# Holding the magnitudes of the first MLP's weights within bounds on GpSimd instead of VectorE

## The chip, the cores and the metric

The program runs on one core of one Trainium2 chip. The metric is the device time of one execution in microseconds; the kernel before has a median of 866.44 us (three runs, 866.27 to 866.68). All times below are microseconds unless they are marked ns.

## The reference

Attention over a window of 64 positions (4 batches, 8 heads, 576 positions, 64 numbers per head), then two MLPs of 512 to 2048 to 512 over the 2304 tokens, with a float32 result. The weights are float64; the kernel gets each number as two 32-bit words and makes float32 of them.

```python
scores = np.where(mask, scale * q @ k.T, -1e9)       # mask: 0 <= row - column < 64
attn = exp(scores - max) / (sum + 1e-9);  x = attn @ v
h = x @ moe_w_in;   x = max(h, 0)**2 @ moe_w_out
h = x @ moe2_w_in;  out = (max(h, 0) + log1p(exp(-abs(h)))) @ moe2_w_out
```

## The kernel before

The attention is cut into 18 pairs of 128 tokens. The first MLP works on five token tiles (384, 384, 512, 512, 512), the second on three of 768. A matmul in full precision is made of three passes: operands are split into a high part and the remainder (a ScalarE copy that rounds, then a VectorE subtraction), and high by high, remainder by high and high by remainder are summed.

The first two tiles of the first MLP use the weights directly, 16 chunks f of w_in and 16 of w_out. A block "L1" (function l1, lines 841 to 844) is the 12 matmuls of one chunk of w_in on one tile, a block "K" (line 863) the 12 of one chunk of w_out. TensorE takes L1 of tile 0, K of tile 0, L1 of tile 1 and the attention's matmuls in a written order. The later tiles use sums of quarter matrices (line 1074) that are loaded back from DRAM.

Every chunk of weights is made ready by add_weights, once for each matrix half f and kind (0 for w_in, 1 for w_out), in eight jobs: load (DMA), magnitude on ScalarE (line 498: absolute value of the upper words as floats), hold on VectorE (line 501: minimum with HUGE, maximum with TINY, in place on the tile z, 128x512), shift (505), top (511), bottom (517), all VectorE, then hi on ScalarE (524) and lo on VectorE (528), which leaves the weight tile w ready for TensorE. Tile names hold f and the kind: w_10_1 is chunk 10 of w_out, w_2_0 chunk 2 of w_in. There are 32 such chunks for the first MLP (ph = 0) and 32 for the second (ph = 1).

The order on each engine is made before anything runs by the class Plan. Each job has an engine with a cost, jobs that it follows, and a due time; due times run backwards from the users and are moved by the table SHIFT, by groups of jobs. A list scheduler then lets each engine take the ready job with the earliest due time, each engine on its own. Some small jobs may go to either of two engines. The engines then run their queues strictly in that order.

Of the kernel before, what the change touches and what calls it, by code (L numbers as in the profile page):

```python
# [16 lines left out]
ALU = mybir.AluOpType  # L17
# [13 lines left out]
    "l0": -0.14, "p0": 71.5, "c0": -0.55, "l1": -0.14, "p1": 54.45, "e1": 0.1, "l2": -0.14, "p2": 74.96, "c2": 0.12,  # L31
    "l3": -0.14, "p3": 100.33, "c3": 0.12, "l4": -0.14, "v4": -0.25, "p4": 135.81, "e4": -0.73, "c4": 0.12,
    "l5": -0.14, "v5": -0.25, "p5": 118.77, "c5": 0.12, "l6": -0.14, "v6": -0.25, "p6": 45.02, "c6": 0.12,
    "l7": -0.14, "v7": -0.96, "p7": 20.52, "c7": 0.12, "l8": -0.14, "v8": -0.25, "p8": 11.17, "c8": 0.12, "l9": -0.14,
    "v9": -0.25, "p9": -4.28, "k9": -0.36, "c9": 0.12, "l10": -0.28, "p10": 37.13, "c10": 0.12, "l11": -0.28,
    "p11": 80.95, "c11": 0.12, "l12": -0.28, "v12": -0.19, "p12": 80.69, "k12": 0.04, "c12": 0.12, "l13": -0.28,
    "v13": -0.19, "p13": 78.46, "c13": 0.12, "l14": -0.93, "v14": -0.19, "p14": 67.37, "c14": 0.12, "l15": 0.28,
    "v15": -0.19, "p15": 96.15, "c15": 0.12, "l16": -0.01, "v16": 1.42, "p16": -38.05, "e16": 1.1, "c16": 0.12,
    "l17": 0.28, "v17": -0.19, "p17": 9.62, "c17": 0.12, "u_0_0": -1.02, "W0_0_0": 154.07, "u_1_0": -1.02,
    "u_0_1": -0.98, "g_0_1": -0.6, "W0_1_0": 193.04, "u_2_0": -1.02, "g_2_0": -2.33, "W0_0_1": 162.23, "u_1_1": -1.02,  # L40
    "g_1_1": -0.6, "u_3_0": -1.02, "g_3_0": -0.6, "u_2_1": -1.02, "g_2_1": -1.24, "W0_1_1": -146.3, "u_4_0": -3.21,
    "g_4_0": -1.24, "W0_0_2": -16.31, "u_3_1": -1.02, "g_3_1": -1.24, "u_5_0": -1.02, "u_4_1": -1.02,
    "W0_1_2": -96.68, "u_6_0": -1.02, "W0_0_3": 160.08, "u_5_1": -1.71, "u_7_0": -1.02, "u_6_1": -1.02,
    "W0_1_3": -72.22, "u_8_0": 0.25, "W0_0_4": 120.95, "u_7_1": -1.02, "u_9_0": -0.43, "u_8_1": -0.43,
    "W0_1_4": -37.64, "u_10_0": -3.02, "W0_0_5": -91.79, "u_9_1": -0.43, "u_11_0": -1.02, "u_10_1": -1.02,
    "W0_1_5": 120.18, "u_12_0": -1.02, "W0_0_6": -5.97, "u_11_1": 0.15, "u_13_0": -1.02, "u_12_1": -1.02,
    "W0_1_6": 230.47, "u_14_0": -0.26, "W0_0_7": 157.36, "u_13_1": -1.02, "u_15_0": -1.02, "u_14_1": -1.02,
    "W0_1_7": 325.52, "u_15_1": -1.02, "S0_0": -110.83, "S0_1": -44.6, "S0_2": -140.65, "S0_3": 152.29,
    "S0_4": -39.95, "S0_5": 9.78, "S0_6": -74.99, "S0_7": 145.26, "L0_0_0": -43.69, "G0_0_0": -0.92, "K0_0_0": 14.31,
    "L0_0_1": -94.54, "G0_0_1": -0.92, "K0_0_1": 123.1, "L0_0_2": 68.92, "G0_0_2": -1.02, "K0_0_2": 33.8,  # L50
    "L0_0_3": 121.83, "G0_0_3": -1.38, "K0_0_3": 162.91, "L0_0_4": 239.43, "G0_0_4": -2.06, "K0_0_4": 162.77,
    "L0_0_5": -95.13, "G0_0_5": -0.92, "K0_0_5": 67.09, "L0_0_6": -81.03, "G0_0_6": -0.41, "K0_0_6": 73.88,
    "L0_0_7": -26.46, "G0_0_7": 26.98, "K0_0_7": 208.31, "R0": -32.49, "L0_1_0": -34.78, "K0_1_0": 86.2,
    "L0_1_1": 167.88, "K0_1_1": -5.89, "L0_1_2": 17.91, "K0_1_2": -27.02, "L0_1_3": 72.74, "G0_1_3": -6.65,
    "K0_1_3": 14.9, "L0_1_4": 92.91, "G0_1_4": 0.05, "K0_1_4": 56.56, "L0_1_5": 77, "G0_1_5": 0.33, "K0_1_5": 336.59,
    "L0_1_6": 22.1, "G0_1_6": 0.33, "K0_1_6": 154.04, "L0_1_7": 173.98, "G0_1_7": -3.34, "K0_1_7": 133.05,
    "R1": 17.25, "W1_0_0": 61.58, "S1_0": 19.49, "W1_1_0": 80.16, "W1_0_1": -9.89, "S1_1": 56.76, "W1_1_1": 102.2,
    "W1_0_2": -7.52, "S1_2": 98.8, "W1_1_2": -30.34, "W1_0_3": -17, "S1_3": -67.82, "W1_1_3": 8.21, "W1_0_4": -103.05,
    "S1_4": 146.2, "W1_1_4": 14.02, "W1_0_5": -17.23, "S1_5": -70.65, "W1_1_5": 72.55, "W1_0_6": -38.03,
    "S1_6": 24.85, "W1_1_6": -19.17, "W1_0_7": 7.38, "S1_7": -55.64, "W1_1_7": 154.65, "X0_2": 10.83, "ri0": -3.61,  # L60
    "ro0": 166.84, "P0_2_0": 5.03, "C0_2_0": -1.56, "G0_2_0": 0.71, "K0_2_0": -20.22, "ri1": 18.82, "ro1": 109.55,
    "P0_2_1": 212, "C0_2_1": -1.48, "K0_2_1": 205.81, "ri2": 25.94, "ro2": 177.03, "P0_2_2": 156.22, "C0_2_2": -1.76,
    "G0_2_2": -4.72, "K0_2_2": 148.43, "ri3": 87.08, "ro3": 141.62, "P0_2_3": 322.35, "C0_2_3": 0.29, "G0_2_3": -4.72,
    "K0_2_3": 57.85, "ri4": 79.03, "ro4": 227.07, "P0_2_4": 99.23, "C0_2_4": 0.22, "G0_2_4": -5.38, "K0_2_4": 114.58,
    "ri5": 59.44, "ro5": 198.08, "P0_2_5": -3.21, "C0_2_5": 0.08, "G0_2_5": -0.09, "K0_2_5": -0.98, "ri6": 88.02,
    "ro6": 182.8, "P0_2_6": 163.84, "C0_2_6": 0.08, "G0_2_6": -0.09, "K0_2_6": 113.09, "ri7": 138.86, "ro7": 138.68,
    "P0_2_7": 263.74, "C0_2_7": 0.08, "G0_2_7": -0.09, "K0_2_7": 181.21, "R2": 54.8, "X0_3": 370.32, "P0_3_7": 39.05,
    "K0_3_7": 179.31, "P0_3_6": 141.27, "C0_3_6": -0.31, "K0_3_6": 37.31, "ri10": 113.65, "P0_3_5": 145.56,
    "K0_3_5": -20.44, "ri11": 40.86, "ro11": 55.48, "P0_3_4": 87.56, "G0_3_4": -1.31, "K0_3_4": 26.13, "ri12": 51.84,
    "ro12": 92.26, "P0_3_3": 148.65, "C0_3_3": 0.38, "G0_3_3": -0.99, "K0_3_3": 76.68, "ri13": 22.67, "ro13": 73.47,  # L70
    "P0_3_2": 257.35, "G0_3_2": -0.25, "K0_3_2": 131.88, "ri14": 113.04, "ro14": 60.62, "P0_3_1": 273.45,
    "C0_3_1": -8.82, "G0_3_1": -0.63, "K0_3_1": 300.68, "ri15": 118.91, "ro15": -13.89, "P0_3_0": 289.5,
    "C0_3_0": -8.88, "G0_3_0": -0.64, "K0_3_0": 212.9, "R3": -62.15, "X0_4": 164.51, "P0_4_0": 46.91, "C0_4_0": 0.05,
    "G0_4_0": -0.05, "K0_4_0": 251.79, "P0_4_1": 7.59, "C0_4_1": 1.64, "G0_4_1": -0.05, "K0_4_1": 147.06,
    "ri18": 112.24, "P0_4_2": 160.66, "C0_4_2": 0.56, "G0_4_2": 0.4, "K0_4_2": 1.32, "ri19": 91.23, "ro19": 5.74,
    "P0_4_3": -12.99, "C0_4_3": 0.68, "G0_4_3": 0.4, "K0_4_3": 67.73, "ri20": 112.66, "ro20": 19.04, "P0_4_4": 143.6,
    "C0_4_4": 0.68, "G0_4_4": 0.09, "K0_4_4": -71.32, "ri21": 117.7, "ro21": 102.77, "P0_4_5": 158.38,
    "C0_4_5": -0.84, "G0_4_5": -0.05, "K0_4_5": -47.88, "ri22": 46.58, "ro22": 63.61, "P0_4_6": 136.85,
    "C0_4_6": -2.13, "G0_4_6": 0.36, "K0_4_6": -52.62, "ri23": 27.7, "ro23": 67.19, "P0_4_7": -119.64,
    "C0_4_7": -4.22, "G0_4_7": 2.59, "K0_4_7": 231.35, "R4": 254.02, "x0": 78.58, "X1_0": 258.41, "ri24": 15.07,  # L80
    "ro24": 58, "P1_0_0": -21.24, "C1_0_0": -0.08, "G1_0_0": -0.08, "K1_0_0": -127.63, "ri25": 102.16, "ro25": 26.91,
    "P1_0_1": -88.26, "C1_0_1": -0.08, "G1_0_1": -0.08, "K1_0_1": -121.22, "ri26": 79.46, "ro26": 72.96,
    "P1_0_2": -133.34, "C1_0_2": -0.42, "G1_0_2": 0.53, "K1_0_2": -52.62, "ri27": 120.66, "ro27": 123.66,
    "P1_0_3": -10.81, "C1_0_3": -0.29, "G1_0_3": -0.29, "K1_0_3": -149.5, "ri28": 82.64, "ro28": 250.42,
    "P1_0_4": -225.28, "C1_0_4": -0.13, "G1_0_4": 0.46, "K1_0_4": 30.76, "ri29": 165.89, "ro29": 237.13,
    "P1_0_5": -200.27, "C1_0_5": -0.32, "G1_0_5": -0.29, "K1_0_5": -124.26, "ri30": 151.82, "ro30": 216.72,
    "P1_0_6": -188.21, "C1_0_6": 0.67, "G1_0_6": -0.29, "K1_0_6": -99.09, "ri31": 72.83, "ro31": 145.11,
    "P1_0_7": -187.94, "C1_0_7": -0.13, "G1_0_7": -4.98, "K1_0_7": 115.18, "x1": 162.42, "X1_1": 175.58,
    "P1_1_7": 52.38, "C1_1_7": -0.29, "G1_1_7": -0.83, "K1_1_7": -135.96, "ri33": -142.49, "P1_1_6": 29.25,
    "C1_1_6": -0.27, "G1_1_6": -1.62, "K1_1_6": -61.31, "ri34": -44.65, "ro34": -103.9, "P1_1_5": 67.4,  # L90
    "C1_1_5": 0.17, "G1_1_5": -1.62, "K1_1_5": -87.06, "ri35": -8.37, "ro35": 187.94, "P1_1_4": 9.88, "C1_1_4": -0.24,
    "G1_1_4": -2.11, "K1_1_4": -54.4, "ri36": 4.75, "ro36": 184.88, "P1_1_3": 77.08, "C1_1_3": -0.9, "G1_1_3": -1.62,
    "K1_1_3": -102.93, "ri37": 143.68, "ro37": 162.68, "P1_1_2": 92.1, "C1_1_2": -0.73, "G1_1_2": -1.06,
# [1428 lines left out]
```

## Time and profile before

| | |
|---|---|
| median of three runs | 866.44 us |
| profiled execution, own time | 868.16 us |
| its span, first to last instruction | 866.4 us |
| TensorE (PE) matmul busy | 850.8 us (98%) |
| VectorE (DVE) busy | 724.2 us (84%) |
| ScalarE (ACT) busy | 616.3 us (71%) |
| GpSimd (POOL) busy | 3.6 us |
| granted TensorE clock, mean | 0.998 |

The profiled execution's own time is 1.7 us above the median, and 1.8 us lie around its span. Busy shares are averages over stages: the first 36 us, in which the attention of the first pairs runs and the first weights arrive, look unlike the rest. A matmul's recorded duration is longer than the spacing of matmuls, since they are pipelined; a block of 12 is read from one block's start to the next one's.

### The profile page before, as it was taken

What the parts mean: (1) busy time and instruction counts of PE and PEld (TensorE: products, weight loads), DVE (VectorE), ACT (ScalarE), POOL (GpSimd) and SP (SyncE); (2) the same over time, 40 slices, a digit from 0 to 9 for tenths busy, and PEclk for the clock granted to TensorE, in tenths of its full rate; (3) what the DMA queues carried; (4) which work ended last, traced back from release to release, by engine and by line L of the source; (5) the groups of instructions that cost most, each with busy time, mean ns of one, the idle gap of its engine ahead of it and who ended that gap; (6) DMA issues with size and microseconds to landing.
All of it is one profiled execution on the core that took longest, in us unless ns stands there. A gap on an engine that the chain in (4) does not pass through costs nothing.

```text
span 866.4 us, 16055 instructions
## 1 busy us (share of the span) xinstructions
PE 850.8 (98%) x5688; PEld 770.1 (89%) x5688; DVE 724.2 (84%) x1389; ACT 616.3 (71%) x1413; POOL 3.6 (0%) x19
## 2 busy tenths in 40 slices
PE   8899999999999999999999999999999999999998
PEld 6699999999988998898999888888889898899896
DVE  6999998798799998899467999999876678776675
ACT  7997776674678676675445888888776678676675
POOL 1000000000000000000000000000000000000000
PEclk9999999999999999999999999999999999999999
DMA  9999866999999899997999999894756551664521
GB/s 214 299 304 368 308 236 213 301 314 312 383 246 334 244 367 289 316 341 260 337 346 353 329 315 335 325 340 153 231 177 205 170 193 40 204 208 161 191 101 73
DMA packets 158575, 225.97 MB, mean 261 GB/s; under 512 B 64544, under 2 KB 115744, under 8 KB 158496
## 3 DMA queue, kind: packets, MB, share of 16 engines
q1 hardware_dynamic: 158496, 224.96, 79.3%
q8 instruction: 45, 0.74, 0.3%
q14 instruction: 34, 0.28, 0.1%
HBM read 169.35 MB, written 55.57 MB: 260 GB/s over the span
## 4 chain that ended last, share of the span: by engine, by line
PE 80%; DVE 8%; DMA 6%; SPq 3%; issue 1%; ACT 1%; DVEq 0%; ACTq 0%
PE acc L863 20%; PE acc L886 20%; PE pa L1074 16%; PE pb L1074 7%; PE pd L1074 5%; PE h L841 2%; PE h L842 2%; PE h L844 2%; SPq L643 2%; PE po L745 2%; DMA raw<-in_moe_w_in_dram 2%; PE pp L726 1%; SPq L474 1%; PE sc L682 1%; DVE gl L914 1%
## 5 line engine op out<-in xcount | busy, mean ns | idle before, releaser
L886 PE MATMUL acc<-ro,gh 128*128 128x512 f32 x576 | 178.9, 391 | 0.0
L886 PEld LDWEIGHTS acc<-ro,gh 128*128 128x128 f32 x576 | 107.2, 188 | 18.6
L863 PE MATMUL acc<-gh,ro 128*128 128x512 f32 x384 | 120.4, 395 | 0.0
L886 PE MATMUL acc<-ro,gl 128*128 128x512 f32 x288 | 113.8, 395 | 0.0
L863 PEld LDWEIGHTS acc<-gh,ro 128*128 128x128 f32 x384 | 69.1, 188 | 13.0 <-issue 0.7
L863 PE MATMUL acc<-gl,ro 128*128 128x512 f32 x192 | 74.9, 390 | 0.0
L914 DVE TENSOR_TENSOR gl<-l,gh 128x384 fp32r<-128x384 f32 x96 | 53.1, 553 | 23.3 <-ACT gh L911 22.4
L911 ACT CAST gh<-l 128x384 fp32r<-128x384 f32 x96 | 48.7, 507 | 24.6 <-DVE l L1261 10.6
L863 PE MATMUL acc<-gh,w 128*128 128x384 f32 x256 | 66.0, 338 | 0.0
L886 PEld LDWEIGHTS acc<-ro,gl 128*128 128x128 f32 x288 | 54.0, 188 | 11.7 <-DVE gl L914 0.3
L1074 PE MATMUL pa<-hxT,ri 128*128 128x384 f32 x288 | 62.0, 336 | 0.0
L1074 PE MATMUL pb<-xT,ri 128*128 128x256 f32 x432 | 60.6, 285 | 0.2 <-DVE wk L1116 0.2
L1257 DVE SCALAR_TENSOR_TENSOR e<-u,e 128x384 f32<-128x384 f32 x96 | 52.8, 550 | 6.2 <-ACT u L1247 6.2
L1074 PEld LDWEIGHTS pb<-xT,ri 128*128 128x128 f32 x432 | 55.9, 191 | 2.0 <-DVE wk L1116 0.4
L1261 DVE TENSOR_TENSOR l<-l,e 128x384 f32<-128x384 f32 x96 | 52.9, 553 | 4.2 <-ACT e L1243 0.5
L1074 PEld LDWEIGHTS pa<-hxT,ri 128*128 128x128 f32 x288 | 51.7, 188 | 2.8
L1252 ACT ACTIVATE l<-u 128x384 f32<-128x384 f32 x96 | 50.3, 524 | 2.7 <-DVE u L1249 1.4
L1074 PE MATMUL pa<-xA,ri 128*128 128x256 f32 (+1 forms) x288 | 51.1, 313 | 0.8 <-ACT c L434 0.6
L1243 ACT ACTIVATE e<-e 128x384 f32<-128x384 f32 x96 | 50.3, 524 | 1.8
L1178 ACT COPY wk<-pa 128x384 f32<-128x384 f32 x72 | 34.2, 475 | 22.8 <-PE pa L1074 22.7
L1074 PEld LDWEIGHTS pa<-xA,ri 128*128 128x128 f32 x288 | 45.3, 189 | 4.1 <-ACT c L434 0.9
L1239 ACT ACTIVATE e<-c 128x384 f32<-128x384 f32 x61 | 31.9, 523 | 23.5 <-DVE c L1186 22.6
(240 smaller groups left out, 2014.1 us busy)
## 6 DMA issues: line engine op xcount, KB each, us to landing
ri<-di SPq DMA_DIRECT2D x126, 512.0 KB, 5.6
ro<-do SPq DMA_DIRECT2D x76, 512.0 KB, 5.4
ri<-di SPq DMA_DIRECT2D x42, 256.0 KB, 3.9
raw<-in_moe_w_in_dram SPq DMA_DIRECT2D x16, 512.0 KB, 9.0
raw<-in_moe_w_out_dram SPq DMA_DIRECT2D x16, 512.0 KB, 6.7
do<-w SPq DMA_DIRECT2D x16, 512.0 KB, 5.3
di<-osa SPq DMA_DIRECT2D x32, 256.0 KB, 6.1
di<-osb SPq DMA_DIRECT2D x32, 256.0 KB, 6.1
```

The source lines that it names most:

```text
L643: nc.sync.dma_start(out=t[done:done + n], in_=src[b, :, s:s + n, :].rearrange("h p d -> p h d"))
L863: nc.tensor.matmul(o, lh, rh, start=n == 0 and k == 0, stop=n == NF - 1 and k == 2)
L886: nc.tensor.matmul(o, lh, rh, start=begins and k == 0, stop=ends and k == 2)
L911: nc.scalar.copy(out=place(j, f"gh{me}", [P, T], F32R), in_=live[src])
L914: nc.vector.tensor_tensor(out=place(j, f"gl{me}", [P, T], F32R), in0=live[src], in1=f32(live[f"gh{me}"]), op=ALU.subtract)
L1074: nc.tensor.matmul(out, w[:, s, c, :], x[k][:, c, :], start=(i == 0 and not on), stop=(i == 5), skip_group_check=on)
L1178: nc.scalar.copy(out=live[f"wk{me}"][:, i], in_=live[f"pa{me}"])
L1239: nc.scalar.activation(out=e, in_=live[src], func=AF.Abs)
L1243: nc.scalar.activation(out=e, in_=e, func=AF.Exp, scale=-1.0)
L1252: nc.scalar.activation(out=live[f"l{me}"], in_=live[f"u{me}"], func=AF.Ln)
L1257: nc.vector.scalar_tensor_tensor(out=e, in0=u, scalar=1.0, in1=e, op0=ALU.subtract, op1=ALU.subtract)
L1261: nc.vector.tensor_tensor(out=live[f"l{me}"], in0=live[f"l{me}"], in1=live[f"e{me}"], op=ALU.add)
```

## The change

The hold of the first MLP's 32 chunks goes to GpSimd, with a planned cost of 1.0; the second MLP's stay on VectorE. The table SHIFT has new numbers throughout, so that all engines' orders change. Lines of the kernel after are 10 or 11 higher than of the kernel before.

```diff
 SHIFT = {
-    "l0": -0.14, "p0": 71.5, "c0": -0.55, "l1": -0.14, "p1": 54.45, "e1": 0.1, "l2": -0.14, "p2": 74.96, "c2": 0.12,
+    "l0": -3.29, "v0": -3.48, "p0": 74.2, "k0": -4.57, "e0": -2.64, "c0": -0.47, "l1": 7.42, "v1": -0.92, "p1": 68.17,
...
         def hold(j):
-            nc.vector.tensor_scalar(out=live[z], in0=live[z], scalar1=HUGE, scalar2=TINY, op0=ALU.min, op1=ALU.max)
+            e = nc.gpsimd if j.who == "POOL" else nc.vector
+            e.tensor_scalar(out=live[z], in0=live[z], scalar1=HUGE, scalar2=TINY, op0=ALU.min, op1=ALU.max)
...
-        add(f"B{me}", {"DVE": 0.34}, hold, [f"A{me}"])
+        add(f"B{me}", {"DVE": 0.34} if ph else {"POOL": 1.0}, hold, [f"A{me}"])
```

VectorE before, where the weights w_9_1 and w_10_1 are made ready (z holds the magnitudes, raw the loaded words, gl the remainder of an activation that a K block reads):

```order
L501 TENSOR_SCALAR z_10_1_1477<-z_10_1_1477 128x512
L914 TENSOR_TENSOR gl_0_9_1487<-prow_13_122,gh_0_9_1481 128x384
L505 TENSOR_SCALAR z_10_1_1477<-z_10_1_1477 128x512
L528 TENSOR_TENSOR w_9_1_1485<-z_9_1_1416,w_9_1_1485 128x512
L511 SCALAR_TENSOR_TENSOR z_10_1_1477<-raw_10_1_1413,z_10_1_1477 128x512
L928 TENSOR_TENSOR area<-area 128x384
L517 SCALAR_TENSOR_TENSOR z_10_1_1477<-raw_10_1_1413,z_10_1_1477 128x512
L505 TENSOR_SCALAR z_14_0_1419<-z_14_0_1419 128x512
L501 TENSOR_SCALAR z_15_0_1507<-z_15_0_1507 128x512
L914 TENSOR_TENSOR gl_0_10_1532<-prow_14_121,gh_0_10_1525 128x384
L511 SCALAR_TENSOR_TENSOR z_14_0_1419<-raw_14_0_835,z_14_0_1419 128x512
L528 TENSOR_TENSOR w_10_1_1530<-z_10_1_1477,w_10_1_1530 128x512
```
Each chunk has its hold (501) and shift (505) on VectorE, and the subtraction of w_10_1 (528) is VectorE's instruction number 200 of the program.

VectorE after, ahead of the same subtraction of w_10_1 (its line is now 539, the shift's 516):

```order
L939 TENSOR_TENSOR area<-area 128x384
L522 SCALAR_TENSOR_TENSOR z_11_1_1454<-raw_11_1_1384,z_11_1_1454 128x512
L925 TENSOR_TENSOR gl_0_10_1492<-prow_14_121,gh_0_10_1488 128x384
L528 SCALAR_TENSOR_TENSOR z_11_1_1454<-raw_11_1_1384,z_11_1_1454 128x512
L516 TENSOR_SCALAR z_10_1_1467<-z_10_1_1467 128x512
L516 TENSOR_SCALAR z_14_0_1482<-z_14_0_1482 128x512
L522 SCALAR_TENSOR_TENSOR z_10_1_1467<-raw_10_1_1337,z_10_1_1467 128x512
L539 TENSOR_TENSOR w_11_1_1512<-z_11_1_1454,w_11_1_1512 128x512
L528 SCALAR_TENSOR_TENSOR z_10_1_1467<-raw_10_1_1337,z_10_1_1467 128x512
L925 TENSOR_TENSOR gl_0_11_1535<-prow_15_120,gh_0_11_1509 128x384
L522 SCALAR_TENSOR_TENSOR z_14_0_1482<-raw_14_0_889,z_14_0_1482 128x512
L539 TENSOR_TENSOR w_10_1_1538<-z_10_1_1467,w_10_1_1538 128x512
```
No hold is left on this engine; the subtraction of w_10_1 is its instruction number 189. Of the instructions up to it, 27 holds are gone, and others have come ahead of it: 4 sums of two weight parts, 4 differences of quarters of them, 2 scalings of q, 3 squares, 1 activation's remainder, and one or two more steps of weights.

GpSimd after, the first holds and the two before and behind w_3_1's:

```order
L397 AFFINE_SELECT masks<-masks 64x64 x12
L512 TENSOR_SCALAR z_2_0_426<-z_2_0_426 128x512
L512 TENSOR_SCALAR z_0_0_464<-z_0_0_464 128x512
L512 TENSOR_SCALAR z_3_0_468<-z_3_0_468 128x512
L512 TENSOR_SCALAR z_1_0_546<-z_1_0_546 128x512
L512 TENSOR_SCALAR z_0_1_613<-z_0_1_613 128x512
L512 TENSOR_SCALAR z_1_1_636<-z_1_1_636 128x512
L512 TENSOR_SCALAR z_2_1_744<-z_2_1_744 128x512
L512 TENSOR_SCALAR z_3_1_776<-z_3_1_776 128x512
L512 TENSOR_SCALAR z_4_0_852<-z_4_0_852 128x512
L512 TENSOR_SCALAR z_10_0_944<-z_10_0_944 128x512
```
GpSimd's queue, which ended with the masks before, now holds 32 of these in the order of the weights; each waits for ScalarE's magnitude, and VectorE's shift of the same chunk waits for it.

TensorE before, where the L1 block of chunk 5 on tile 1 (h_1_5) ends:

```order
L842 MATMUL h_1_5_1464<-xh_1_830,w_5_0_1088 128x384
L844 MATMUL h_1_5_1464<-xl_1_831,w_5_0_1088 128x384 x4
L863 MATMUL acc_0_0_912<-gh_0_8_1411,w_8_1_1460 128x384 x2
L863 MATMUL acc_0_0_912<-gl_0_8_1421,w_8_1_1460 128x384
L863 MATMUL acc_0_1_916<-gh_0_8_1411,w_8_1_1460 128x384 x2
L863 MATMUL acc_0_1_916<-gl_0_8_1421,w_8_1_1460 128x384
```
It stands ahead of the K block of w_8_1.

TensorE after, where that L1 block begins:

```order
L874 MATMUL acc_0_2_789<-gh_0_12_1592,w_12_1_1594 128x384 x2
L874 MATMUL acc_0_2_789<-gl_0_12_1596,w_12_1_1594 128x384
L874 MATMUL acc_0_3_793<-gh_0_12_1592,w_12_1_1594 128x384 x2
L874 MATMUL acc_0_3_793<-gl_0_12_1596,w_12_1_1594 128x384
L852 MATMUL h_1_5_1655<-xh_1_892,w_5_0_1039 128x384
L853 MATMUL h_1_5_1655<-xh_1_892,w_5_0_1039 128x384
```
It now stands behind the K block of w_12_1. Up to the first matmul on w_10_1 TensorE has 20 L1 blocks and 10 K blocks before, and 19 L1 and 10 K after, with the same attention work. Up to the first matmul on w_3_1 it has 9 L1 and 3 K blocks and 25 groups of transpositions before, and 4 L1, 3 K and 24 groups after.

## Rows read from the trace of the kernel before

**Rows 1.** The page: span, busy time of each engine, chain by engine

```profile
span 866.4 us, 16055 instructions
...
PE 850.8 (98%) x5688; PEld 770.1 (89%) x5688; DVE 724.2 (84%) x1389; ACT 616.3 (71%) x1413; POOL 3.6 (0%) x19
...
PE 80%; DVE 8%; DMA 6%; SPq 3%; issue 1%; ACT 1%; DVEq 0%; ACTq 0%
```

**Rows 2.** Stretches: busy us and instructions of each engine, PEclk, DMA share, GB/s

```profile
0.00:14.00 14.00, 11.99 (x134) 9.38 (x138) 6.08 (x13) 7.96 (x26) 3.59 (x19) 1.00 1.08 208
14.00:36.00 22.00, 17.24 (x248) 13.82 (x239) 20.89 (x44) 20.26 (x85) 0.00 (x0) 0.92 1.03 243
36.00:108.00 72.00, 69.77 (x507) 67.29 (x508) 71.84 (x146) 60.48 (x136) 0.00 (x0) 1.00 1.00 332
300.00:600.00 300.00, 297.18 (x1913) 265.86 (x1912) 261.20 (x494) 211.28 (x448) 0.00 (x0) 1.00 0.93 320
```

**Rows 3.** VectorE in order: start us, duration us, line, operation, tiles [idle before <-releaser]

```profile
43.40 0.68 DVE L698 TENSOR_REDUCE nm<-sc 128x4 f32<-128x512 f32 x1
44.00 0.68 DVE L511 SCALAR_TENSOR_TENSOR z<-raw,z 128x512 uint32<-128x512 uint32 x1
44.60 0.42 DVE L501 TENSOR_SCALAR z<-z 128x512 f32<-128x512 f32 x1
44.93 0.68 DVE L517 SCALAR_TENSOR_TENSOR z<-raw,z 128x512 uint32<-128x512 uint32 x1
...
68.03 0.67 DVE L528 TENSOR_TENSOR w<-z,w 128x512 fp32r<-128x512 f32 x1
...
105.74 0.54 DVE L914 TENSOR_TENSOR gl<-prow,gh 128x384 fp32r<-128x384 f32 x1
106.20 0.67 DVE L511 SCALAR_TENSOR_TENSOR z<-raw,z 128x512 uint32<-128x512 uint32 x1
106.81 0.67 DVE L528 TENSOR_TENSOR w<-z,w 128x512 fp32r<-128x512 f32 x1
```

**Rows 4.** The chain in order of time: start us, us, what

```profile
65.58 2.08 PE acc L863 x12
67.66 0.17 PE h L841
...
69.74 2.08 PE acc L863 x12
...
107.62 0.44 PE tq L654 x4
108.06 2.11 PE acc L863 x12
```

**Rows 5.** VectorE in order, the idle times of the start

```profile
6.32 0.69 DVE L434 COPY kT<-tk 128x512 f32<-128x512 f32 x1 [3.30 <-PE tk L654]
8.67 1.29 DVE L698 TENSOR_REDUCE nm<-sc 128x4 f32<-128x512 f32 x2 [1.66 <-PE sc L682]
11.18 0.29 DVE L434 COPY kT<-kT 128x256 f32<-128x256 f32 x1 [1.23 <-PE sc L682]
```

**Rows 6.** GpSimd: groups by line, count | busy us, mean ns of one

```profile
L387 POOL TENSOR_SCALAR_AFFINE_SELECT masks<-masks 64x64 bf16<-64x64 bf16 x12 | 2.5, 236 | 0.3
masks.py:199 POOL TENSOR_SCALAR_AFFINE_SELECT ident<-ident 128x128 f32<-128x128 f32 x1 | 0.3, 292 | 0.1
```

**Rows 7.** Groups of VectorE by line and shape, count | busy us, mean ns of one

```profile
L501 DVE TENSOR_SCALAR z<-z 128x512 f32<-128x512 f32 x53 | 21.6, 414 | 4.7 <-ACT z L498 4.7
L501 DVE TENSOR_SCALAR halvesw<-halvesw 128x512 f32<-128x512 f32 x11 | 4.6, 418 | 0.3 <-ACT halvesw L498 0.2
```

**Rows 8.** TensorE's waits from 300 to 600 us: us in total, times, longest

```profile
PE tq L654 <- DVE k L719: 0.9, 1, 0.9
PE pa L1074 <- ACT c L434: 0.6, 1, 0.6
```

**Rows 9.** A stretch of the start, columns as in rows 2

```profile
30.00:34.00 4.00, 3.55 (x11) 3.04 (x12) 3.97 (x9) 2.48 (x7) 0.00 (x0) 0.57 1.01 323
```

154 rows, old and new, of the table SHIFT are left out of this document.

## The prediction

> **What bounds the kernel now.** The page comes first: TensorE is busy for 98% of the span and makes up 80% of the chain of waits [rows 1]. It does the same matmuls before and after, so the time can move only by stretches in which TensorE waits. The busy times by stretches show where these are: TensorE misses 2.0 us of the first 14, 4.8 from 14 to 36 and 2.2 from 36 to 108 [rows 2], and 2.8 from 300 to 600, which the waits put down to single late tiles [rows 2, 8]. In the same stretches VectorE idles 7.9 us, then 1.1, then 0.2 of 72 [rows 2]. So from 14 us until the first MLP's weights are ready VectorE never rests, and TensorE runs just behind it. The rows of VectorE and of the chain side by side show how close: the subtraction that finishes w_3_1 starts at 68.03 and ends 0.67 later, its K block starts at 69.74; for w_10_1 it is 106.81 + 0.67 = 107.48 against 108.06 [rows 3, 4]. What reaches VectorE ahead of these points later than now, by more than 0.6 to 1.0 us, makes TensorE wait, and nothing behind gives that back. What reaches it sooner is worth little, since TensorE misses only 2.2 of the 72 us there.
>
> **The change part by part.** All durations are start to start, because VectorE begins an instruction before the last one's recorded end. A hold takes 0.33 (44.60 to 44.93; 0.335 over many), a 128x512 operation with two tiles 0.60 (44.00 to 44.60), a 128x384 one 0.46 (105.74 to 106.20) [rows 3]. The trace has 64 holds, 53 + 11 [rows 7]; half of them are the first MLP's and leave VectorE, 32 x 0.33 = 10.6 us.
>
> How much of this helps is read where TensorE waits for VectorE. Up to and with the subtraction of w_10_1 VectorE has 201 instructions before. Summed by kind: 56 of 0.335, 115 of 0.60, 13 of 0.47, 12 reciprocals of 0.20 and five small ones of 1.2 together, 97.7 us; the instruction ends at 107.48, so 9.7 us of that time were idle or start-up. After, it has 190: 33, 124, 17, 12 and four, 97.1 us. The 27 holds that are gone (9.0 us) are nearly made up by the operations that the new order puts ahead of this point. TensorE meanwhile has one L1 block less ahead of it, and a block is 2.08 (67.66 to 69.74) [rows 4], so at its present pace it asks for w_10_1 at 108.06 - 2.08 = 105.98. At w_3_1 the sums are 59.0 us (122 instructions) before and 50.4 (100) after, and TensorE has five L1 blocks and one group of transpositions (0.44) less ahead: it asks at 69.74 - 10.84 = 58.9 [rows 4].
>
> With the same 9.7 us of idle time VectorE finishes w_10_1 at 106.8 and w_3_1 at 60.1, 0.9 and 1.2 us after TensorE asks. The idle time can shrink: 6.2 us of it are three waits for the first transposition and scores [rows 5], which stand in the same order after, and 7.9 is what idles before 14 us [rows 2]. With 7.9 it finishes at 105.0 and 58.3, and TensorE waits no more than now. So the new order by itself costs between 0 and 1.2 us; I take 0.7, the middle.
>
> The other unknown is the hold on GpSimd, which the trace does not show. Its duration: GpSimd's 64x64 select takes 236 ns and its 128x128 one 292 ns [rows 6]; 56 ns per 64 numbers in a row give 292 + 6 x 56 = 628 ns for 512, an estimate. The growth alone gives 0.45, and the dearer reading, 292/128 ns for each number, gives 1.17. What it does to VectorE can lie between nothing (the two run beside each other) and its whole duration (one waits until the other is done). Behind the shift that waits for the hold stand the other steps of several weights and the remainders (line 914) that K blocks need, so what VectorE loses there TensorE loses too.
>
> I take a loss near the upper end, for what VectorE's own rows show. A one-tile operation on SBUF, the hold, puts 512 numbers through in 0.33, while the reduction that reads 512 from PSUM takes 0.60, as long as an operation that reads 2 x 512 from SBUF [rows 3]. So both the fast form and the two-tile form bring SBUF numbers in at twice the rate of the reduction; they use a second way in, and GpSimd's hold has to read and write the same memory. In the order after, 70 of the 78.5 us that VectorE works between the first weight and w_10_1, 0.89, are such operations. 27 holds stand ahead of w_10_1; the first six, ahead of w_1_1's, I count as hidden, since VectorE still idles there (1.1 us from 14 to 36 [rows 2]) and a quarter of its work there reads PSUM. 21 x 0.63 x 0.89 = 11.8 us. With 0.7 from the order that is 12.5, on top of 866.4.
>
> The Trainium skill says it outright ("SBUF — State Buffer", section "Who interferes with whom"): VectorE and GpSimd share one pair of ports as an exclusive lock, taken by a fast one-tile operation or, against a GpSimd instruction that reads SBUF, by one with two SBUF inputs, and the other engine blocks for the whole instruction. No run here shows it yet. Its "GPSIMD Engine Reference", section "Elementwise — side-by-side cycle accounting", gives 769 ns for 512 numbers in a tight loop; by that the same sum would be 0.7 + 21 x 0.77 x 0.89 = 15.1 us.
>
> The rest costs nothing by itself. ScalarE's magnitude and rounding steps are the same in number; it idles 11.5 us of the 72 [rows 2], which covers the ten jobs that it takes over in the whole program. The end of the program has the same last matmuls, copies and stores. The profiled execution took 868.16, its span 866.4, and the median is 866.44; I add to the median, since the profiled one carries 1.7 us more than the runs.
>
> **The rivals.** *They run beside each other* (27%). For it: the new order's cost is small, and while VectorE cleared kT at the start GpSimd's selects took no longer than otherwise; but clearing reads nothing. Then only the order counts, 0 to 1.2, and the late waits may move by one either way: 867.1, from 865 to 869.
>
> *The late waits go* (13%), the case on the other side. TensorE misses 2.8 us between 300 and 600 [rows 2], 0.9 for one pair's probabilities, 0.6 for a copied activation piece and smaller ones [rows 8]. The new table puts these stages in another order as well, and if it happens to set those pieces sooner, with the holds free and the start as it was, the time is 866.4 - 2.8 = 863.6. It decides from 1.7 us regained on. Against it: in these stages VectorE is at 87% and the waits are single tiles, which a new order moves about as easily as it removes them.
>
> *They take turns* (60%) is the forecast. Its own range: 21 holds of 0.45 with the order free, 21 x 0.45 x 0.89 = 8.4, hence 875; all 27 at 1.0 and the order's 1.2 give 28, hence 894.
>
> **How the numbers follow.** The likeliest time is 866.4 + 12.5 = 878.9, own range 875 to 894. The range for 8 in 10 must take in the second case and leaves out most of the third: 864.6 to 893. A kernel's runs here spread by 0.05%, and about 0.2% (1.7 us) is what can be told from no change. Slower than 868.1: the 60 and a fifth of the 27, together 66%. Within 864.7 to 868.1: three quarters of the 27, 20%. Faster: the 13 and 1 of the 27, 14%.
>
> **What would show it right or wrong.** Right: GpSimd's 32 holds last 0.5 to 0.8 us start to end or longer, VectorE's two-tile operations or its shifts show gaps of 0.3 us and more right where a hold runs, and TensorE's waits between 40 and 130 us grow to more than 10 us, on w or gl of VectorE; the time behind 165 us is as before. Wrong in the mechanism: VectorE's operations keep 0.60 and 0.33 while holds run. Wrong in the order: TensorE's missing time before 130 us changes by less than 1.5 us or shrinks. A granted clock that falls again counts against the sum as well: from 30 to 34 us it was 0.57 behind a stretch of waits [rows 9], which cost 4 x 0.43 = 1.7 us, and more waits there could cost it twice.

## The result, and the profile after

The changed kernel takes 875.54 us (median of 4 runs, 874.86 to 877.69), the kernel before beside it 866.56: 1.0101 of before, 95% interval 1.0085 to 1.0117, so 7.4 to 10.1 us slower. 878.9 was forecast, own range 875 to 894. The profiled execution of the changed kernel took 877.69, the longest of its four; what is read from its trace carries some 2 us more than the median.

The page after, as in [rows 1]:

```profile
span 875.9 us, 16061 instructions
...
PE 854.9 (98%) x5688; PEld 769.8 (88%) x5688; DVE 720.7 (82%) x1347; ACT 618.9 (71%) x1423; POOL 34.3 (4%) x51
...
PE 69%; DVE 17%; issue 4%; DMA 4%; ACT 2%; SPq 2%; POOL 2%; DVEq 0%; POOLq 0%; ACTq 0%
```

TensorE is still busy 98%: its busy time for the same 5688 matmuls grew from 850.8 [rows 1] to 854.9 us, and its missing time from 15.6 to 21.0, which together make the 9.5 us by which the span grew. Its share of the chain has gone from 80% to 69% and VectorE's from 8% to 17%. VectorE has 42 instructions fewer (1347 for 1389: 32 holds, and ten jobs that went to ScalarE), and yet its busy time falls by 3.5 us only. The stretches of [rows 2] after:

```profile
0.00:14.00 14.00, 11.09 (x122) 8.41 (x126) 6.72 (x14) 7.91 (x28) 3.59 (x19) 1.00 1.07 207
14.00:36.00 22.00, 16.60 (x224) 12.91 (x219) 19.21 (x38) 18.23 (x71) 2.62 (x4) 0.85 1.07 261
36.00:108.00 72.00, 65.52 (x495) 60.28 (x487) 70.66 (x124) 54.88 (x132) 20.11 (x21) 1.00 0.92 301
300.00:600.00 300.00, 299.85 (x1951) 269.98 (x1950) 256.94 (x481) 212.26 (x451) 0.00 (x0) 1.00 0.93 317
```

Between 36 and 108 us TensorE now misses 6.5 us where it missed 2.2, and VectorE gets 124 instructions done where it did 146. Between 300 and 600 the 2.8 us of single waits are down to 0.15. What happens where a hold runs is seen with VectorE's and GpSimd's rows side by side (start us, duration us). GpSimd first, three holds: one beside VectorE's reductions of scores, which read PSUM (nm<-sc, from 37.54 to 38.8), and two beside work of VectorE on SBUF:

```profile
37.53 0.61 POOL L512 TENSOR_SCALAR z<-z 128x512 f32<-128x512 f32 x1 [3.80 <-ACT z L508]
...
60.07 0.89 POOL L512 TENSOR_SCALAR z<-z 128x512 f32<-128x512 f32 x1 [3.80 <-ACT z L508]
...
86.78 3.64 POOL L512 TENSOR_SCALAR z<-z 128x512 f32<-128x512 f32 x1 [3.67 <-ACT z L508]
```

VectorE in the same places:

```profile
59.81 0.68 DVE L528 SCALAR_TENSOR_TENSOR z<-raw,z 128x512 uint32<-128x512 uint32 x1
60.42 1.09 DVE L522 SCALAR_TENSOR_TENSOR z<-raw,z 128x512 uint32<-128x512 uint32 x1
61.43 0.68 DVE L770 TENSOR_TENSOR xl<-po,xh 128x512 fp32r<-128x512 f32 x1
...
86.06 0.68 DVE L539 TENSOR_TENSOR w<-z,w 128x512 fp32r<-128x512 f32 x1
86.66 0.68 DVE L528 SCALAR_TENSOR_TENSOR z<-raw,z 128x512 uint32<-128x512 uint32 x1
87.26 0.54 DVE L925 TENSOR_TENSOR gl<-prow,gh 128x384 fp32r<-128x384 f32 x1
87.73 0.41 DVE L516 TENSOR_SCALAR z<-z 128x512 uint32<-128x512 uint32 x1
88.06 1.28 DVE L581 TENSOR_TENSOR z<-w 128x512 f32<-128x512 f32 x2
89.27 0.68 DVE L539 TENSOR_TENSOR w<-z,w 128x512 fp32r<-128x512 f32 x1
90.46 0.43 DVE L516 TENSOR_SCALAR z<-z 128x512 uint32<-128x512 uint32 x1 [0.51 <-POOL z L512]
```

GpSimd's group of the 32 holds (count | busy us, mean ns of one | idle before it):

```profile
L512 POOL TENSOR_SCALAR z<-z 128x512 f32<-128x512 f32 x32 | 30.7, 969 | 94.9 <-ACT z L508 88.7 <-DVE sm L728 6.2
```

A hold that meets no conflict, as the one beside the reductions, lasts 0.61. The one at 60.07 stretches VectorE's next operation from 0.68 to 1.09 and the distance to the one behind it from 0.60 to 1.01: 0.41 lost. The one at 86.78 is itself kept out for about 3 us: VectorE works on without a gap until its next instruction is the shift that needs this very hold, and then idles 0.51 for it. The mean of 969 ns is such waiting on top of 0.61.

### The profile page after: what moved, and what is told of

It is laid out like the page before. It is cut to its first block, busy times and chain, and to the rows that moved or that the text cites. A ratio compares the mean times of both kernels' runs of the same rounds, so it can differ in the third digit from the quotient of the medians.

```text
span 875.9 us, 16061 instructions
## 1 busy us (share of the span) xinstructions
PE 854.9 (98%) x5688; PEld 769.8 (88%) x5688; DVE 720.7 (82%) x1347; ACT 618.9 (71%) x1423; POOL 34.3 (4%) x51
## 4 chain that ended last, share of the span: by engine, by line
PE 69%; DVE 17%; issue 4%; DMA 4%; ACT 2%; SPq 2%; POOL 2%; DVEq 0%; POOLq 0%; ACTq 0%
PE acc L874 18%; PE acc L897 16%; PE pa L1085 15%; PE pb L1085 8%; PE pd L1085 4%; DVE z L522 2%; PE po L756 2%; POOL z L512 2%; DVE gl L925 2%; SPq L654 2%; DVE z L528 1%; PE pp L737 1%; DVE e L1268 1%; DVE z L516 1%; PE sc L693 1%
## 5 line engine op out<-in xcount | busy, mean ns | idle before, releaser
L874 PE MATMUL acc<-gh,w 128*128 128x384 f32 x256 | 68.7, 344 | 6.2 <-DVE w L539 4.4
L874 PEld LDWEIGHTS acc<-gh,w 128*128 128x128 f32 x256 | 45.7, 188 | 9.7 <-DVE w L539 6.9
```

Of the source, the lines that this page charges most:

```text
L874: nc.tensor.matmul(o, lh, rh, start=n == 0 and k == 0, stop=n == NF - 1 and k == 2)
```

## The experiments

My theory: the hold costs VectorE about as much time on GpSimd as it did on VectorE itself, because the two exclude each other, and the new order has already spent that time on other work. Rivals: latency (the weights come late since GpSimd is slow and there are two handovers more), and the order alone. The kernel before was run beside each series (medians 867.6 to 868.8 there), so ratios to it are compared; 0.001 is 0.87 us. In the table "short" is a hold cut to 8 of its 512 columns, and "aside" a GpSimd instruction for whose result nobody waits. In the edits "..." stands for arguments left out, and "ident (x4)" for the constant tile ident read four times over.

| kernel | hold | us | ratio to before (95%) |
|---|---|---|---|
| before | VectorE | 866.56 | 1 |
| old order, without (e6) | none | 868.25 | 0.9999 (0.9983 to 1.0015) |
| old order, GpSimd (e4) | GpSimd | 869.19 | 1.0018 (1.0006 to 1.0029) |
| old order, twice (e11) | VectorE, 2x | 881.97 | 1.0158 (1.0139 to 1.0177) |
| old order, GpSimd aside (e10) | VectorE, and GpSimd aside | 873.21 | 1.0055 (1.0034 to 1.0076) |
| after | GpSimd | 875.54 | 1.0101 (1.0085 to 1.0117) |
| new order, without (e1) | none | 866.32 | 0.9977 (0.9967 to 0.9987) |
| new order, short (e2) | GpSimd, 8 columns | 867.19 | 0.9989 (0.9979 to 0.9998) |
| new order, aside (e3) | short, and aside | 875.60 | 1.0086 (1.0070 to 1.0101) |
| new order, aside twice (e8) | short, and 2x aside | 885.46 | 1.0206 (1.0187 to 1.0225) |
| new order, memset aside (e9) | short, and 3 memsets | 872.36 | 1.0054 (1.0036 to 1.0071) |
| new order, VectorE (e5) | VectorE | 875.71 | 1.0090 (1.0059 to 1.0121) |
| old start, new end (e7) | VectorE | 866.46 | 0.9985 (0.9972 to 0.9999) |

**e1: the new order without the holds.**

```diff
-            e = nc.gpsimd if j.who == "POOL" else nc.vector
-            e.tensor_scalar(out=live[z], in0=live[z], scalar1=HUGE, scalar2=TINY, op0=ALU.min, op1=ALU.max)
+            if ph:
+                nc.vector.tensor_scalar(out=live[z], ...)
```

> The changed kernel with the holds of the first MLP left out altogether (its weights' magnitudes are not bounded); order and moments as in the changed kernel. By turn-taking (GpSimd's hold and VectorE's operations exclude each other): the stall goes with the holds, what is left is the order's own 0 to 1.2 us less up to 2.7 us of late waits, so 864 to 867. By latency (the weights come later because the hold on GpSimd lasts 0.6 to 1.0 us and is handed over twice): the same, 864 to 867. By the order alone (the new moments themselves cost it): 873 to 876, hardly below the changed kernel.

866.32 us, 0.9977 of before. Without the holds the new order costs nothing, so the new moments by themselves are not the cause; what the order costs with the holds in it, e5 shows. The waits of the K blocks, TensorE's lines by form in the stretch 14 to 130 us, of e1:

```profile
L874 PE MATMUL acc<-gh,w 128*128 128x384 f32 x126 | 33.1, 341 | 1.4 <-DVE w L539 1.4
```

and of the changed kernel:

```profile
L874 PE MATMUL acc<-gh,w 128*128 128x384 f32 x112 | 31.0, 347 | 6.1 <-DVE w L539 4.3 <-ACT gh L922 1.3 <-ACT w L535 0.4
```

The K blocks wait 1.4 us for w without holds and 4.3 with them; by 130 us they have done 112 of these matmuls instead of 126.

**e2 and e3: the handover without the occupation, and the occupation without the wait.** e2 cuts the hold to 8 columns; e3 adds an instruction of the old length on constant tiles.

```diff
+            t = live[z] if ph else live[z][:, 0:8]
+            e.tensor_scalar(out=t, in0=t, ...)
+            if not ph:                                  # e3 only
+                e.tensor_scalar(out=spare, in0=ident (x4), ...)
```

> The changed kernel with each hold of the first MLP cut to 8 of its 512 columns (the others are not bounded): GpSimd still stands in the chain between ScalarE and VectorE, both handovers stay, only the time it holds the memory goes. By turn-taking: 864 to 868. By latency through the handovers: 870 or more; by latency through the hold's length alone: 864 to 868. By the order alone: 873 to 876.

> As the run with the short holds, and behind each short hold GpSimd does the same two-operation instruction on 512 numbers of constant tiles (reads 512 fp32, writes 512 bytes) that nobody waits for. The weights are not bounded beyond 8 columns. By turn-taking: VectorE is blocked as often and as long as in the changed kernel, 872 to 877, and VectorE's two-tile operations read about 1.0 us beside it instead of 0.6. By latency: as the short holds, 864 to 868, since no step waits for the long instruction.

e2 takes 0.9989 of before, about 1 us over e1: two handovers and the 8 columns cost next to nothing. e3 takes 1.0086, as much as the changed kernel within the intervals, though no step waits for the result of its long instruction. The next short hold stands behind it in GpSimd's queue, but VectorE idles only 0.3 us ahead of its shifts between 36 and 130 us (the row of L524 under e9). So latency falls too; what costs is that the long instruction runs beside VectorE's. VectorE's engine line says by how much. The page of e1:

```profile
PE 849.6 (98%) x5688; PEld 769.7 (89%) x5688; DVE 712.6 (82%) x1347; ACT 619.8 (72%) x1423; POOL 3.6 (0%) x19
```

The page of e3:

```profile
PE 852.7 (98%) x5688; PEld 769.5 (88%) x5688; DVE 723.9 (83%) x1347; ACT 620.0 (71%) x1423; POOL 42.5 (5%) x83
```

The same 1347 instructions of VectorE take 11.3 us more, 0.35 for each of the 32. In the changed kernel the idling for holds comes to it, in the row of VectorE's shifts between 36 and 130 us:

```profile
L516 DVE TENSOR_SCALAR z<-z 128x512 uint32<-128x512 uint32 x27 | 12.7, 475 | 2.6 <-POOL z L512 2.6
```

It is 720.7 - 712.6 = 8.1 of lengthening and 2.6 of idling, 10.7 or 0.33 each. That is the price of a hold on VectorE, 0.335 [rows 3, 7].

**e8: the instruction aside twice** (edit against e3).

```diff
             e.tensor_scalar(out=spare, in0=ident (x4), ...)
+            e.tensor_scalar(out=spare, in0=ident (x4), ...)
```

> As the run with the instruction aside, but two such instructions on 512 numbers behind each short hold; the weights are not bounded beyond 8 columns. If blocking by GpSimd is what the time goes to, the 9.3 us over the run without holds double: 866.3 + 18.6 = 885, from 882 to 888, and VectorE's busy time grows by some 22 us over 712.6. If only the fact counts that GpSimd interferes at the weight's moment, not for how long, it stays at 875 to 878.

885.46, or 1.0206 of before: 0.0229 over e1, where e3 is 0.0109 over it. VectorE's line on the page:

```profile
PE 855.8 (97%) x5688; PEld 773.0 (87%) x5688; DVE 734.0 (83%) x1347; ACT 620.0 (70%) x1423; POOL 69.8 (8%) x115
```

It is busy for 21.4 us more than in e1, against 11.3 in e3. Both doubled, as turn-taking has it.

**e9: GpSimd only writes** (edit against e3).

```diff
-            e.tensor_scalar(out=spare, in0=ident (x4), ...)
+            nc.gpsimd.memset(spare, 1)                  # three times
```

> As the run with the instruction aside, but what GpSimd does behind each short hold only writes: three memsets of 512 bytes in each partition, with nothing read from SBUF. The weights are not bounded beyond 8 columns. If VectorE's two-tile operations are blocked by a GpSimd instruction that reads and writes, but not by one that only writes, they keep 0.68 us, only the one-tile shift can lengthen, and the time is 866 to 869. If any long GpSimd instruction blocks them, VectorE's busy time grows as it did beside the reading instruction (some 0.3 us and more for each weight) and the time is 873 to 878.

VectorE by form between 36 and 130 us, of e3:

```profile
L530 DVE SCALAR_TENSOR_TENSOR z<-raw,z 128x512 uint32<-128x512 uint32 x28 | 21.2, 764 | 0.2
L536 DVE SCALAR_TENSOR_TENSOR z<-raw,z 128x512 uint32<-128x512 uint32 x27 | 21.2, 789 | 0.1
...
L524 DVE TENSOR_SCALAR z<-z 128x512 uint32<-128x512 uint32 x27 | 13.1, 491 | 0.3
```

and of e9:

```profile
L535 DVE SCALAR_TENSOR_TENSOR z<-raw,z 128x512 uint32<-128x512 uint32 x29 | 19.7, 680 | 0.1
L529 DVE SCALAR_TENSOR_TENSOR z<-raw,z 128x512 uint32<-128x512 uint32 x29 | 19.6, 682 | 0.2
...
L523 DVE TENSOR_SCALAR z<-z 128x512 uint32<-128x512 uint32 x28 | 17.1, 613 | 1.1 <-POOL z L515 0.7
```

Beside GpSimd instructions that read, the two-tile steps that stand where GpSimd's instruction comes grow to 764 and 789 ns (684 to 686 in e1). Beside those that only write they stay at 680, and the one-tile shift alone grows, from 420 to 613. The expected mechanism is there, but its price was missed: 193 ns on each shift make 872.36, between the two forecasts. The Trainium skill has both halves ("SBUF — State Buffer", section "Who interferes with whom"): an operation with two SBUF inputs is in conflict with a GpSimd instruction that reads SBUF, not with one that only writes it, and a fast one-tile form with either. The trace agrees in both. That the engine which comes second waits for the whole instruction, as the section also says, is more than the rows show: 0.41 us lost to a hold of 0.61.

**e5: the new order, the hold back on VectorE.**

```diff
-            e = nc.gpsimd if j.who == "POOL" else nc.vector
+            e = nc.vector
```

> The changed kernel's order on every engine, word for word, but each hold of the first MLP runs on VectorE, at the place in the program where GpSimd's stood. If what counts is VectorE's time, 0.335 us for a hold of its own against the 0.36 by which VectorE's busy time grew for each long GpSimd instruction beside it (723.9 less 712.6 over 32), then this takes as long as the changed kernel: 873 to 877. If GpSimd's own slowness or the handovers were the cost, it falls towards the run without holds: 866 to 870.

875.71: as long as on GpSimd. Which engine does the hold makes no difference in this order; that the moments were chosen as if VectorE had these 10.6 us free does. Without holds the order is 0.9977, with them, on either engine, 1.009 to 1.010. So the new order is no cost only as long as nobody has to do the holds: with them left on VectorE, where the kernel before has them, it costs 0.0090, 7.8 us.

**e4, e6 and e11: the old order with the hold on GpSimd, left out, and done twice.**

```diff
-            nc.vector.tensor_scalar(out=live[z], ...)
+            (nc.vector if ph else nc.gpsimd).tensor_scalar(out=live[z], ...)   # e4
+            if ph: nc.vector.tensor_scalar(out=live[z], ...)                   # e6
+            nc.vector.tensor_scalar(out=live[z], ...)   # e11: the old line, and again if not ph
```

> The kernel before with its own moments and order on every engine; only the instruction itself goes to GpSimd, so VectorE's queue loses 32 holds and the shifts wait for GpSimd. By turn-taking: each hold takes 0.335 us from VectorE and gives it 0.4 to 0.63 of blocking, 27 x 0.07 to 0.3 us more ahead of w_10_1, 868 to 875. By latency: in the old order the shift stands two or three operations behind the hold, so VectorE's queue head waits for GpSimd nearly every time, some 0.3 to 1.0 us each: 875 to 890. Beside each other, with no handover price: 866 or less, by the 10.6 us of VectorE's holds at most 857.

> The kernel before with the first MLP's holds left out (magnitudes not bounded), order otherwise its own. VectorE gets 10.6 us back, 9.0 of them ahead of w_10_1. If the old order with GpSimd's hold came out even because blocking took what the move freed, this is clearly faster than the kernel before: TensorE misses 7.0 us between 14 and 108, so 3 to 6 us less. If the start is bound by arrivals (DMA, the first scores) and not by VectorE's sum, it is within 1 us of the kernel before.

> The kernel before, complete and in its own order, with every hold of the first MLP done twice on VectorE (the second changes nothing): 32 x 0.335 = 10.7 us more on VectorE, 9.0 of them ahead of w_10_1, and no work on GpSimd. The run without holds (10.6 us less on VectorE, 0.9999 of the kernel before) leaves two readings. If VectorE stands just at its edge, what is taken away gains nothing but what is added counts: 6 to 9 us more than the kernel before, 1.007 to 1.010. If VectorE has slack on both sides of where it stands, within 2 us of the kernel before.

e4 takes 1.0018 of before. VectorE's line on its page:

```profile
PE 849.9 (98%) x5688; PEld 768.4 (89%) x5688; DVE 724.1 (84%) x1357; ACT 615.8 (71%) x1413; POOL 31.8 (4%) x51
```

The move by itself costs 1.6 us (0.5 to 2.5 by the interval): VectorE's busy time is 724.1 (724.2 before [rows 1]) with 32 instructions fewer, so blocking took all that the move gave. Latency's 875 to 890 is refuted a second time. With e5 this tells the two parts of the change apart: in either order the hold's engine makes 0.001 to 0.002, and most of the 1.0101 comes from an order that has no room for the holds on either engine.

e6 shows that in the old order nothing was to be gained anyway: the holds' 10.6 us off VectorE change nothing, where I had expected 3 to 6 us less if blocking was all that kept e4 from gaining. Stretches of e6:

```profile
36.00:60.00 24.00, 21.94 (x220) 19.71 (x221) 21.97 (x43) 22.78 (x66) 0.00 (x0) 0.93 1.06 328
60.00:80.00 20.00, 20.00 (x118) 20.00 (x117) 18.81 (x35) 15.64 (x32) 0.00 (x0) 1.00 0.97 308
80.00:108.00 28.00, 28.00 (x164) 28.00 (x163) 24.92 (x47) 20.75 (x41) 0.00 (x0) 1.00 0.91 326
```

The last two of before:

```profile
60.00:80.00 20.00, 20.00 (x118) 20.00 (x117) 20.00 (x41) 15.76 (x31) 0.00 (x0) 1.00 1.01 329
80.00:108.00 28.00, 28.00 (x166) 27.96 (x165) 28.00 (x57) 21.15 (x41) 0.00 (x0) 1.00 0.93 328
```

VectorE, busy for 71.84 of these 72 us before [rows 2], now rests 6.3, and TensorE does no better, since from 60 us it was full already: 20.00 of 20 and 28.00 of 28 before. The other way, e11's 10.7 us more on VectorE cost 13 (1.0158), more than the 6 to 9 that I expected and more than the 10.7 themselves; why, no run shows. The same stretch, 36 to 130 us, of e11:

```profile
36.00:130.00 94.00, 85.09 (x594) 79.04 (x593) 92.16 (x191) 66.61 (x146) 0.00 (x0) 0.97 0.87 281
```

TensorE misses 8.9 us there (2.2 before), at a lower clock besides (from 14 to 36 us it is the other way round, 0.99 for 0.92 before). A fully busy VectorE stood just at its edge.

**e10: GpSimd aside in the old order.**

```diff
             nc.scalar.copy(out=live["w" + me][:, 0], in_=live[z])
+            if not ph:
+                nc.gpsimd.tensor_scalar(out=gate, in0=(first 8 columns of w), ...)
+                nc.gpsimd.tensor_scalar(out=spare, in0=ident (x4), ...)
```

> The kernel before, complete, with its holds on VectorE; in addition GpSimd does, behind each rounding step of a first-MLP weight, an 8-column instruction that reads it and then the instruction on 512 numbers of constant tiles, which nobody waits for. VectorE loses some 0.36 us for each, 11.4 in all. If VectorE stands just at its edge in the old order (busy 71.84 of 72 us), every us taken from it now counts: 867.8 + 7 to 10 = 875 to 878. If the old order has slack there, as its run without holds could mean (VectorE 10.6 us lighter, no gain), 868 to 871.

873.21, below what the edge predicts; but the load did not come where I meant it, and VectorE's busy time grew by 6.6 us (730.8) and not by 11.4. GpSimd's rows:

```profile
63.97 57.83 POOL L529 TENSOR_SCALAR gate<-w 128x8 f32<-128x8 f32 x1 [1.38 <-ACT w L527]
121.77 0.61 POOL L532 TENSOR_SCALAR spare<-ident 128x512 uint8<-128x512 f32 x1
```

and VectorE's where this ends:

```profile
120.87 0.54 DVE L925 TENSOR_TENSOR gl<-g,gh 128x384 fp32r<-128x384 f32 x1
121.33 0.41 DVE L508 TENSOR_SCALAR z<-z 128x512 uint32<-128x512 uint32 x1
121.67 0.67 DVE L702 TENSOR_TENSOR k<-sc,masks 128x512 f32<-128x512 f32 x1
```

An 8-column instruction of 0.19 us stood for 57.83. So this run did not test the edge, and e11 was made for it.

**e7: the old start with the new end.** Holds on VectorE; the ranks change from the old to the new table when the planner's clock passes 240 us.

```diff
+            if later and now >= SWITCH:
+                for k, j in self.jobs.items():
+                    j.rank = later[k]
```

> The kernel before, holds on VectorE, with its own order up to the planner's time 240 us; from there the ranks come from the new table. The computation is complete. If the 2.8 us of single waits between 300 and 600 us go because of the new late moments, 863 to 865.5 on a chip where the kernel before takes 866.5 (2 to 3 less than the kernel before). If the new late moments only fit the new early ones, no gain, or waits elsewhere: 0 to 2 us more.

0.9985, some 1.3 us less than before and not the 2 to 3 that I expected: the fastest complete kernel here, by about as much as can be told at all. Its missing time between 300 and 600 us is 0.9 (2.8 before, 0.15 after), so two thirds of the late waits came along.

## Why the prediction was right, and where not

Its direction and mechanism held: the two engines take turns, and TensorE pays for it. By its own terms:

**The bound** was read rightly: TensorE just behind VectorE, little to gain from sooner, all to lose from later. e6 and e11 show both sides. One step was too narrow: that the time can move only by stretches in which TensorE is read as missing. Of the 9.5 us by which the span grew, 4.1 are longer busy time for the same matmuls; no run shows how much of that is waits and how much the clock.

**The price of the holds**, 11.8 us, was too high. The estimate of 628 ns for one was good (610). But a hold that meets VectorE takes 0.41 from it, not 0.89 of 0.63 (0.56), and one that is kept out takes almost nothing until VectorE must wait for it. Over 32 holds VectorE lost 10.7 us, 0.33 each; the kernel lost 1.0101 - 0.9977, about 10.8 us (9.2 by the medians, 875.54 less 866.32). That 11.8 comes so near is in part luck: a price too high met a count too low, and 21 holds at 0.33 would have made 7.0. The other sum, 15.1, went by the 769 ns for 512 numbers of the Trainium skill ("GPSIMD Engine Reference", section "Elementwise — side-by-side cycle accounting"). The trace does not agree: the hold here takes 610 ns, and blocks for less than its length.

**The order**, 0.7 us, was wrong in sign as a whole, and wrong in both of its parts. (The middle of 0 to 1.2 is 0.6, and by the prices that it lists the prediction's two sums for VectorE are about 0.2 us lower; neither moves anything.) Without holds the new order is 2.0 us faster than before. By the stretches, TensorE misses 11.1 us up to 130 where it missed 9.0, so the start costs 2.1, above my 0 to 1.2. A stretch of e1, and then of before:

```profile
0.00:130.00 130.00, 118.88 (x1016) 109.64 (x1017) 118.60 (x227) 102.59 (x275) 3.60 (x19) 0.99 0.98 296
```

```profile
0.00:130.00 130.00, 121.00 (x1055) 111.61 (x1056) 120.78 (x245) 105.55 (x288) 3.59 (x19) 0.99 0.96 288
```

The late waits give back 2.7. I had made these a rival that wants the start unharmed, with 13%, and wrote that the time behind 165 us stays as it was. It was no rival but another term: it came true together with the turn-taking, and should have been added to it. So 0.7 + 11.8 = 12.5 became -2.0 + 10.8 = 8.8 (taken from ratios, which add up by construction; the medians differ by 9.0). The kernel before is less steady than the 0.05% of its first three runs: the 25 beside e1 lie between 866.21 and 869.86, so by their intervals these terms hold to 1 to 1.5 us.

**The signs I named.** GpSimd's holds of 0.5 to 0.8 "or longer": 0.61 to 3.64. Gaps in VectorE of 0.3 and more: 0.41, as a longer operation and not as a gap. Waits on w: yes, 4.3 us. "More than 10 us between 40 and 130": 8.2 missing of the 90 (0.6 before), so no. "The time behind 165 us is as before": no, by the late waits. The clock did fall a second time. In the changed kernel it was 0.75 from 18 to 20 us and 0.50 from 20 to 22, after TensorE had been busy for 2.0 of the 4 us from 16 to 20, and again from 32 us on:

```profile
30.00:34.00 4.00, 2.76 (x11) 2.37 (x12) 3.97 (x8) 2.96 (x13) 0.82 (x1) 0.83 1.10 283
34.00:36.00 2.00, 2.00 (x16) 0.86 (x19) 2.00 (x5) 1.97 (x9) 0.00 (x0) 0.50 1.21 242
```

At 0.50 TensorE ran at 1.2 GHz, after waits that left it busy 2.76 of the 4 us before. That is 0.7 + 1.0 us lost there and another 1.7 from 18 to 24, against one fall of 1.7 from 30 to 34 before [rows 9]: twice as dear, as the prediction feared, and so the 0.85 for 0.92 in the stretch from 14 to 36. It is not what makes the kernel slow: e3 and e5 have 0.92 there, as before, and take 875.60 and 875.71. It may be why the profiled execution is 2 us above the median.

**What stays open.** That 2.1 and 2.7 make 0.6 and not the 2.0 by which e1 is faster. The two profiled spans, 866.4 and 864.8, differ by 1.6: TensorE misses 15.6 us in the one and 15.2 in the other, and the remaining 1.2 is its busy time, 850.8 and 849.6 for the same matmuls. Why they take less is not shown.

## What to carry to other kernels

Work moved from VectorE to GpSimd beside a VectorE full of two-tile and fast one-tile operations on SBUF cost VectorE here what it had cost before. An order that is laid out for the freed time then runs late. Before relieving an engine that is busy 100%, take its work out altogether once and add it twice: here the first gave nothing and the second cost 13 us, which says that in that order there is nothing to win, and where the edge is.

## What the runs showed that was not expected

VectorE can keep GpSimd out for 57.83 us. In e10 it did 117 instructions between 64.3 and 121.6, 42 of the fast one-tile form and 75 with two SBUF inputs, without a gap, and GpSimd's small instruction, ready all the time, came through only when VectorE took one that reads PSUM (k<-sc,masks at 121.67). In the changed kernel it cannot last as long, because VectorE's own shift waits for the hold. What exactly lets GpSimd in is not settled: the hold at 60.07 came in between two two-tile operations, with neither an idle time nor a PSUM operand in VectorE's rows.

A VectorE busy 99.8% over 72 us was not what bounded the kernel: e6 took 6 us of that work away and TensorE did not move.
